# Silu moved to the reader's side of a round trip through DRAM, and products on two fixed pairs of PSUM banks

## The chip, the cores and the metric

The kernel runs on one core of a Trainium2 chip. The metric is the device time of one execution in microseconds, the median of several runs. All times below are microseconds unless marked ns.

## The reference

A recurrent linear attention (RetNet), followed by a feed-forward block with Silu. The inputs are float32 arrays for q, k and v (4 batches, 8 heads, 768 steps, 64 wide) and float64 weights, which the kernel converts itself.

```python
gamma = 1.0 - 2.0 ** (-5.0 - np.arange(H))
for t in range(S):
    state = gamma * state + k[:, :, t] (outer) v[:, :, t]
    y[:, :, t] = scale * (q[:, :, t] @ state)
x = y as (B*S, H*D) = (3072, 512)
h = x @ w_in                                  # (3072, 2048)
g = h * (1.0 / (1.0 + np.exp(-h)))            # Silu
out = g @ w_out                               # (3072, 512)
```

## The kernel before, in words

**Numbers.** The two big products are made of three products of fp32r parts each: an operand is split into a high part, a low part and a mixed part, and the sums of the first two and of the third go to two PSUM banks, `ha` and `hb` in the first half, `oa` and `ob` in the second. The result is `ONE_E * ha - hb`.

**Chunks, units, tiles.** The 768 steps are 6 chunks `c` of 128 steps; a unit is a chunk of one of the 4 batches, so there are 24 units. The width 2048 of the hidden layer is 16 slices `f` of 128. A product (c, f) of the first half (`multiply`, L749) multiplies a slice of w_in with the 512 columns (4 batches of 128 steps) of chunk c: 12 matmuls of 128x512, 8 into `ha` and then 4 into `hb` (L754).

**The first half.** The 96 products run in the order of the list `steps` (L1150), which is written out by hand, with the attention's work for the units (`visit` and `halves`, L690 to L739) put behind some of them. The first four products and the visits up to unit 10 or so stand in a hand-written order of their own (L968 to L1137). After a product, `close_steps` (L775) does three things: ACT copies `ha` to a buffer g and scales it (L777), DVE subtracts `hb` (L782), ACT applies Silu in place (L787). Then `put_g` (L792) has SP store g to DRAM (`g_dram`, L797). There are three g buffers (pool `hpool`); nine early products keep their g for longer in free weight slots (`new_g`, L764; their tile is called gk). While all this runs, ACT and DVE also convert and split the weights (L211 to L230, and L121 to L129) and do their part of the visits: xt (L653, L656, L659) is the attention's output, split in three parts, which the products of its chunk read.

**PSUM.** There are 8 banks: two each for the tags s and y, one for q, and three, h0 to h2, that `turn` (L403) hands out in rotation. Before the change `ha` and `hb` take the next two of the rotation. The bank of tag q is used by the transposes of the visits up to unit 13 (`steps_t`, L480), and those also take a turn. Later units are transposed by DMA (`turn_t`, L452; POOL separates the words for it, L444).

**The second half.** For each chunk and each f, `split` (L833) handles a g that SP loaded from DRAM four ahead (`get`, L803, L810): ACT writes the high part (L842), DVE the other two (L844, L845). The parts of four f are one block in a pool of two, so four Copies run together when TensorE has finished the block before the last. `split` runs 3 ahead of the matmuls: 12 of 128x512 per f (L1268), into 8 banks for 4 batches. At the end of a chunk ACT and DVE empty the banks (L1316, L1317), and SP stores the rows (L1244). The loads use 8 buffers in rotation (tags kf, qf and vf), so load n waits for the DVE subtraction (L844) of n - 8.

**What sets the order.** TensorE's order is the program's. On the other engines, from L1138 on, a scheduler orders the instructions; `tc.issue_after(ins)` makes those in its block queue behind `ins` if they are on the same engine. Names used for it: `copied[0]` is the newest L777, `taken_out[0]` the newest L782, `stored[0]` the newest store of a g.

Of the kernel before, what the change touches and what calls it, by code (L numbers as in the profile page):

```python
# [18 lines left out]
AF = mybir.ActivationFunctionType  # L19
# [15 lines left out]
def kernel(  # L35
# [28 lines left out]
    nc = tc.nc  # L64
# [17 lines left out]
    def pool(name, bufs, **kw):  # L82
# [14 lines left out]
    g_dram = {(c, f): dram.tile([128, NT], FP32, tag=f"g{c}_{f}", name=f"gd_{c}_{f}")  # L97
              for c in range(NC) for f in range(NF)}
# [40 lines left out]
    def woven(t, parted=False):  # L139

        if parted:
            return t.rearrange("p (h o n) -> p h n o", h=2, o=2)
        return t.rearrange("p (o n) -> p n o", o=2)
# [118 lines left out]
    def queue(ins):  # L262

        return ExitStack() if written[0] or ins is None else tc.issue_after(ins)
# [54 lines left out]
    def fill(out, n, start=True):  # L319

        cols = out.shape[-1] // 128
        for _ in range(n):
            nc.tensor.matmul(out, lhsT=zero, rhs=zero.unsqueeze(1).to_broadcast([128, cols, 128]),
                             start=start, stop=True, skip_group_check=True)
# [66 lines left out]
    taken_out, copied, masked, fenced = [], [], [], []  # L391
# [6 lines left out]
    def banks(tag, name, n=2):  # L398
        return ps_u.tile([128, n, 512], FP32, tag=tag, name=name)
# [3 lines left out]
    def turn(name):  # L403
        turns[0] += 1
        return ps_h.tile([128, 512], FP32, tag=f"h{turns[0] % 3}", name=name)
# [17 lines left out]
    def scale_k(n):  # L423
        if 0 <= n < len(units):
            t = kqv["k"][n]
            if units[n][0] == NC - 1:
                t = t[:D]
            g = gk[: t.shape[0], units[n][0], :].unsqueeze(2).to_broadcast([t.shape[0], H, D])
            engine = nc.gpsimd if 2 * B + 1 < n < FAR else nc.vector
            engine.tensor_tensor(out=t, in0=t, in1=g, op=ALU.mult)  # L430
# [27 lines left out]
    def join_t(name, n):  # L458

        to, bufs = (qt, 3) if name == "q" else (kt, 2)  # L460
        to[n] = one.tile([128, HP, C], FP32, tag=f"{name}t", name=f"{name}t_{n}", bufs=bufs)
        nc.scalar.copy(out=to[n].bitcast(U16).rearrange("p a (t w) -> p w a t", w=2),
                       in_=turned.pop((name, n)).rearrange("p (w a) t -> p w a t", w=2))
# [279 lines left out]
    apart = [(FAR + 1, "k"), (FAR + 1, "q"), (FAR + 2, "q")]  # L743
    pending, stored = [], []

    def product_in(c, f):
        close_in(c, f, *multiply(c, f))

    def multiply(c, f):  # L749
        ha, hb = turn(f"ha_{c}_{f}"), turn(f"hb_{c}_{f}")  # L750
        fill(ha, FILL_P.get((c, f), 0))
        for i in range(3):
            for kk in range(KIN):
                nc.tensor.matmul(hb if i == 2 else ha, lhsT=w_sb[f][:, i, ts(kk, 128)],  # L754
                                 rhs=woven(xt[c][:, i, kk, :]), start=kk == 0 and i != 1,
                                 stop=kk == KIN - 1 and i != 0)
        return ha, hb
# [6 lines left out]
    def new_g(c, f):  # L764
        if (c, f) not in kept_g:
            return hpool.tile([128, NT], FP32, tag="hs", name=f"g_{c}_{f}")
        i, = (i for i in keep_g if (c, f) in keep_g[i])
        if i not in homes:
            homes[i] = wpool.tile([128, 3, NT], FP32, tag=f"w{i}", name=f"gk_{i}")
        return homes[i][:, keep_g[i].index((c, f))]  # L770

    def close_in(*of):
        list(close_steps(*of))

    def close_steps(c, f, ha, hb):  # L775
        hs = new_g(c, f)
        copied[:] = [nc.scalar.activation(out=hs, in_=ha, func=AF.Copy, scale=ONE_E).ins]  # L777
        with queue(copied[0]):
            while behind_copy:
                behind_copy.pop(0)()  # L780
        yield
        taken_out[:] = [nc.vector.tensor_tensor(out=hs, in0=hs, in1=hb, op=ALU.subtract).ins]  # L782
        with queue(taken_out[0]):
            while behind_next:
                behind_next.pop(0)()
        yield
        nc.scalar.activation(out=hs, in_=hs, func=AF.Silu)  # L787
        (later if (c, f) in kept_g else pending).append((c, f, hs))

    later = []  # L790
# [1 line left out]
    def put_g(keep, of=None):  # L792
        of = pending if of is None else of
        while len(of) > keep:
            c, f, g = of.pop(0)
            with tc.issue_after(last[0]) if of is later else ExitStack():
                last[:] = stored[:] = [nc.sync.dma_start(out=g_dram[c, f], in_=g).ins]  # L797
# [5 lines left out]
    def get(n):  # L803
        if n >= len(order):
            return
        c, f = order[n]
        name = "kvqkvkqv"[n % 8]
        g = ld.tile([128, NT], FP32, tag=f"{name}f", name=f"gr_{c}_{f}",
                    bufs=2 if name == "q" else 3)
        nc.sync.dma_start(out=g, in_=g_dram[c, f])  # L810
        got[n] = g

    def get_w(f):
# [19 lines left out]
    def split(n):  # L833
        if n >= len(order):
            return
        c, f = order[n]
        get(n + G_AHEAD)
        g = got.pop(n)
        if f % 4 == 0:
            blocks[n // 4] = xpool.tile([128, 3, 4, NT], FP32R, tag="xt", name=f"gs_{c}_{f}")  # L840
        t = blocks[n // 4][:, :, f % 4, :]
        nc.scalar.activation(out=t[:, 0, :], in_=g, func=AF.Copy, scale=HALF)  # L842
        high = t[:, 0, :].bitcast(FP32)
        nc.vector.tensor_tensor(out=t[:, 1, :], in0=g, in1=high, op=ALU.subtract)  # L844
        nc.vector.scalar_tensor_tensor(out=t[:, 2, :], in0=t[:, 1, :].bitcast(FP32),  # L845
                                       scalar=-1.0 / EPS, in1=high,
                                       op0=ALU.mult, op1=ALU.add)
        ready[n] = t
# [294 lines left out]
    pairs = [(1, 1), (1, 2), (0, 3), (1, 3), (0, 4), (1, 4)]  # L1143
# [6 lines left out]
    steps = pairs + three + rest + last + groups  # L1150
# [32 lines left out]
    put_later = {6: 1, 7: 2, 9: 1, 10: 1, 11: 1, 13: 1, 14: 1, 15: 1}  # L1183
    assert sum(put_later.values()) == len(kept_g)
    loads_at = {first_far + 4: [("k", FAR + 1), ("q", FAR + 1)], far[FAR] + 1: [("q", FAR + 2)]}
    for n, (c, f) in enumerate(steps):
        if n in scales_at:
            behind_next.append(lambda m=scales_at[n]: scale_k(m))
        if n in joins_at:
            behind_copy.insert(0, lambda m=joins_at[n]: [join_t(name, m) for name in "qk"])  # L1190
        if n in parts:
            behind_next.append(lambda m=parts[n]: part_t(m, taken_out[0]))
        patient[0] = steps.index((3, 0)) <= n < max(turns_at) + 2
        product_in(c, f)
        put_g(1)
        if n in put_later:
            put_g(len(later) - put_later[n], later)
        store_w()
        if (c, f) in takes:
            take_w(taken_out[0], n < len(pairs + three) or c == NC - 1)  # L1200
        behind.get((c, f), lambda: None)()
        if n in turns_at:
            turn_t(turns_at[n])
            if turns_at[n] >= LATER:
                with tc.issue_after(turned_by[0]):
                    load("k", turns_at[n] + 1), load("q", turns_at[n] + 1)
        if turns_at.get(n - 1, 0) >= LATER:
            with tc.issue_after(stored[0]):
                load("v", turns_at[n - 1] + 1)
        if turns_at.get(n - 2, 0) >= LATER:  # L1210
            with tc.issue_after(stored[0]):
                while waiting:
                    load_w(waiting.pop(0))
        for name, m in loads_at.get(n, ()):
            load(name, m)
        if c == NC - 1:
            if f == 0:
                for i in range(W_READ):
                    get_w(i)
            if f < NF - 4:  # L1220
                w_out(f, True)
            if f >= NF - 6:
                if f == NF - 6:
                    for n in range(G_AHEAD):
                        get(n)
                if f >= NF - S_AHEAD:
                    with tc.issue_after(taken_out[0]):
                        split(f - NF + S_AHEAD)
# [6 lines left out]
    def unwoven(t):  # L1235

        return t.rearrange("p (n o) -> p o n", o=2)
# [8 lines left out]
    for c in range(NC):  # L1246
        acc = []
        for b in range(B):
            if b < 2:
                u = banks("sy"[b], f"o{b}_{c}")  # L1250
# [5 lines left out]
        for f in range(NF):  # L1256
            n = c * NF + f
# [3 lines left out]
            t = ready[n]  # L1261
# [13 lines left out]
        if early_f < NF:  # L1275
# [3 lines left out]
                         for x in ("left", "right")]  # L1279
            nc.scalar.activation(out=apart_cols(halves_of[0]),  # L1280
                                 in_=unwoven(acc[B - 1][0][:, left]), func=AF.Copy,
# [16 lines left out]
        for b in range(B):  # L1298
            oa, ob = acc[b]
            if c == NC - 1 and b == B - 1:  # L1300
# [4 lines left out]
                for i, (x, cols, op) in enumerate(((last_left, left, ALU.add),  # L1305
                                                   (oa, right, ALU.subtract))):
                    nc.vector.scalar_tensor_tensor(
                        out=apart_cols(o[i]), in0=unwoven(x[:, cols]), scalar=ONE_E,
# [44 lines left out]
```

## Time and profile before

| | |
|---|---|
| median of 3 runs | 601.49 (600.5 to 601.88) |
| profiled execution | 600.71 |
| its span | 598.7 |
| TensorE busy | 583.7 (97%) |
| VectorE (DVE) busy | 399.6 (67%) |
| ScalarE (ACT) busy | 333.2 (56%) |
| GpSimd (POOL) busy | 34.4 (6%) |
| DMA, share of 16 engines | 64.5% (main queue) |

The profile is of one execution; its span reaches from the first to the last instruction. PE is TensorE's matmuls, PEld its weight loads, which run beside them. A row of the groups gives line, engine, operation, output<-input, shapes and count, then busy time, mean ns of one, idle time of the engine just ahead and what ended it. A row of the timeline gives start, length, engine, line and, in brackets, the wait ahead of it and what ended the wait. A row of the waits gives the total, how often and the longest. Line numbers in rows are those of the kernel before.

### The profile page before, as it was taken

How to read it: one execution, taken by the hardware profiler on the slowest of the kernel's cores; microseconds unless marked ns; L12 is line 12 of the kernel's file. 1: busy time of each engine (PE TensorE's matmuls, PEld its weight loads, DVE VectorE, ACT ScalarE, POOL GpSimd, SP SyncE). 2: the span in 40 equal slices, each digit the busy share in tenths (PEclk: the TensorE clock that was granted, in tenths of full speed). 3: DMA queues.
4: the chain of work that ended last, by engine and by line, in shares of the span. 5: the costliest groups of instructions: out<-in, count | busy, mean ns of one | idle time of the engine just before them, and what ended most of it. 6: DMA issues, size and time to landing. Idle time of an engine off the chain costs nothing. (4 is left out here: it accounts for less than half of the span.)

```text
span 598.7 us, 13719 instructions
## 1 busy us (share of the span) xinstructions
PE 583.7 (97%) x5509; PEld 496.5 (83%) x5509; DVE 399.6 (67%) x672; ACT 333.2 (56%) x607; POOL 34.4 (6%) x89
## 2 busy tenths in 40 slices
PE   8999999999999999999999999999999999999997
PEld 6687887878778788878887888888888888888886
DVE  3888898777887767766679895553735544554632
ACT  7778878777867667777789761412312221413211
POOL 3000220100012111111000000000000000000000
PEclk9999999999999999999999999999999999999999
DMA  9997868785799689999977654352533524442301
GB/s 190 214 212 185 210 177 269 231 249 172 211 268 202 183 251 234 248 267 301 310 242 258 202 158 138 105 175 73 175 107 105 176 78 134 141 139 79 133 1 70
DMA packets 144334, 108.89 MB, mean 182 GB/s; under 512 B 101136, under 2 KB 109584, under 8 KB 144272
## 3 DMA queue, kind: packets, MB, share of 16 engines
q1 hardware_dynamic: 144272, 108.03, 64.5%
q8 instruction: 43, 0.70, 0.5%
q14 instruction: 19, 0.16, 0.1%
HBM read 66.06 MB, written 36.70 MB: 172 GB/s over the span
## 5 line engine op out<-in xcount | busy, mean ns | idle before, releaser
L754 PE MATMUL ha<-xt,wi 128*128 128x512 f32 x736 | 177.8, 384 | 1.0 <-DVE g L782 0.9
L754 PEld LDWEIGHTS ha<-xt,wi 128*128 128x128 f32 x736 | 136.0, 189 | 25.9 <-DVE g L782 6.4
L1268 PE MATMUL o<-wo,gs 128*128 128x512 f32 x564 | 137.1, 379 | 0.0
L842 ACT ACTIVATE gs<-gr 128x512 fp32r<-128x512 f32 x96 | 53.0, 619 | 130.2 <-issue 129.7
L1268 PEld LDWEIGHTS o<-wo,gs 128*128 128x128 f32 x564 | 106.6, 189 | 15.1
L844 DVE TENSOR_TENSOR gs<-gr,gs 128x512 fp32r<-128x512 f32 x96 | 62.3, 687 | 84.9 <-ACT gs L842 84.9
L1268 PE MATMUL oa<-wo,gs 128*128 128x512 f32 x376 | 111.8, 379 | 0.0
L754 PE MATMUL hb<-xt,wi 128*128 128x512 f32 x368 | 95.9, 383 | 4.9 <-ACT g L777 3.6
L782 DVE TENSOR_TENSOR g<-g,hb 128x512 f32<-128x512 f32 x87 | 59.6, 685 | 49.4 <-ACT g L777 46.0
L754 PEld LDWEIGHTS hb<-xt,wi 128*128 128x128 f32 x368 | 68.2, 189 | 19.3 <-ACT g L777 8.0
L1268 PEld LDWEIGHTS oa<-wo,gs 128*128 128x128 f32 x376 | 71.1, 189 | 10.1
L787 ACT ACTIVATE g<-g 128x512 f32<-128x512 f32 x87 | 54.6, 628 | 32.0 <-DVE g L782 31.9
L1268 PE MATMUL ob<-wo,gs 128*128 128x512 f32 x188 | 71.3, 379 | 0.0
L845 DVE SCALAR_TENSOR_TENSOR gs<-gs 128x512 fp32r<-128x512 f32 x96 | 62.2, 686 | 0.1
L777 ACT ACTIVATE g<-ha 128x512 f32<-128x512 f32 x87 | 51.2, 588 | 14.5 <-DMA gd<-g 11.0
L1268 PEld LDWEIGHTS ob<-wo,gs 128*128 128x128 f32 x188 | 35.5, 189 | 5.0
L211 ACT ACTIVATE ca<-wf 128x512 f32<-128x512 f32 x32 | 26.7, 835 | 12.6 <-DVE cs L224 7.0
L1316 ACT ACTIVATE o<-o 128x512 f32<-128x512 f32 x10 | 6.0, 600 | 31.1 <-PE o L1268 30.9
L224 DVE SCALAR_TENSOR_TENSOR cs<-ca,cs 128x512 uint32<-128x512 uint32 x32 | 22.4, 701 | 0.9
L659 DVE SCALAR_TENSOR_TENSOR xt<-xt 128x512 fp32r<-128x512 f32 x28 | 22.1, 800 | 0.6
L542 DVE TENSOR_TENSOR am<-sc,decay 128x512 f32<-128x512 f32 x24 | 16.5, 687 | 8.0 <-PE sc L534 6.9
L582 PE MATMUL y<-qt,mid 64*64 64x64 f32 x376 | 19.4, 220 | 0.6 <-issue 0.6
(137 smaller groups left out, 615.9 us busy)
## 6 DMA issues: line engine op xcount, KB each, us to landing
gr<-gd SPq DMA_DIRECT2D x96, 256.0 KB, 2.8
gd<-g SPq DMA_DIRECT2D x87, 256.0 KB, 3.4
wf<-in_moe_w_out_dram SPq DMA_DIRECT2D x16, 512.0 KB, 5.2
out_dram<-o SPq DMA_DIRECT2D x23, 256.0 KB, 2.5
wf<-in_moe_w_in_dram SPq DMA_DIRECT2D x16, 256.0 KB, 4.0
wf<-in_moe_w_in_dram SPq DMA_DIRECT2D x32, 128.0 KB, 3.9
kf<-in_k_dram SPq DMA_DIRECT2D x16, 256.0 KB, 4.4
qf<-in_q_dram SPq DMA_DIRECT2D x16, 256.0 KB, 4.9
```

The lines of the kernel that those rows point to most:

```text
L211: top = nc.scalar.activation(out=a.bitcast(FP32), in_=hi.bitcast(FP32), func=AF.Abs, scale=2.0 ** -3).ins
L224: nc.vector.scalar_tensor_tensor(out=s, in0=a, scalar=3, in1=s, op0=ALU.logical_shift_left, op1=ALU.bitwise_xor)
L582: i = nc.tensor.matmul(to[ts(e, D), o, a, :], lhsT=lhsT, rhs=rhs, start=key not in started, stop=True, skip_group_check=True).ins
L659: nc.vector.scalar_tensor_tensor(out=x[2], in0=x[1].bitcast(FP32), scalar=-1.0 / EPS, in1=x[0].bitcast(FP32), op0=ALU.mult, op1=ALU.add)
L754: nc.tensor.matmul(hb if i == 2 else ha, lhsT=w_sb[f][:, i, ts(kk, 128)], rhs=woven(xt[c][:, i, kk, :]), start=kk == 0 and i != 1, stop=kk ...
L777: copied[:] = [nc.scalar.activation(out=hs, in_=ha, func=AF.Copy, scale=ONE_E).ins]
L782: taken_out[:] = [nc.vector.tensor_tensor(out=hs, in0=hs, in1=hb, op=ALU.subtract).ins]
L787: nc.scalar.activation(out=hs, in_=hs, func=AF.Silu)
L842: nc.scalar.activation(out=t[:, 0, :], in_=g, func=AF.Copy, scale=HALF)
L844: nc.vector.tensor_tensor(out=t[:, 1, :], in0=g, in1=high, op=ALU.subtract)
L845: nc.vector.scalar_tensor_tensor(out=t[:, 2, :], in0=t[:, 1, :].bitcast(FP32), scalar=-1.0 / EPS, in1=high, op0=ALU.mult, op1=ALU.add)
L1268: nc.tensor.matmul(o, lhsT=g, rhs=woven(wo[f][:, i, :], (c, b) == (NC - 1, B - 1)), start=f == 0 and i != 1, stop=f == NF - 1 and i != 0 o ...
```

## The change

The Silu behind a product's subtraction goes away, so g is stored without it, and the second half applies Silu in place on the loaded g, ahead of the Copy of its high part; it is queued behind the newest copy of the first half. The loads of g are queued behind the newest store of a g. From the product behind unit 13's visit on (the 86 steps after `pairs`), products take their banks by turns: the even ones two of the rotation, the odd ones one of the rotation and the bank of tag q.

```diff
+    home_of = {}
+
     def multiply(c, f):
-        ha, hb = turn(f"ha_{c}_{f}"), turn(f"hb_{c}_{f}")
+        names = f"ha_{c}_{f}", f"hb_{c}_{f}"
+        home = home_of.get((c, f), "t")
+        if home in "sy":
+            u = banks(home, names[0])
+            ha, hb = (u[:, i] for i in range(2))
+        else:
+            ha = turn(names[0])
+            hb = banks("q", names[1], 1)[:, 0] if home == "q" else turn(names[1])
...
     def close_steps(c, f, ha, hb):
...
         yield
-        nc.scalar.activation(out=hs, in_=hs, func=AF.Silu)
         (later if (c, f) in kept_g else pending).append((c, f, hs))
...
     def get(n):
...
-        nc.sync.dma_start(out=g, in_=g_dram[c, f])
+        with tc.issue_after(stored[0]):
+            nc.sync.dma_start(out=g, in_=g_dram[c, f])
...
     def split(n):
...
         t = blocks[n // 4][:, :, f % 4, :]
+        with tc.issue_after(copied[0]):
+            nc.scalar.activation(out=g, in_=g, func=AF.Silu)
         nc.scalar.activation(out=t[:, 0, :], in_=g, func=AF.Copy, scale=HALF)
...
+    home_of.update({x: "tq"[n % 2] for n, x in enumerate(steps[len(pairs) :])})
     for n, (c, f) in enumerate(steps):
```

The homes s and y, which `multiply` can also take, are given to no product here.

## Prediction

> **What bounds the kernel now.** I read the stage table first (busy time of each engine in stretches; its clock column stands before the DMA share).
>
> ```profile
> 80.00:345.50 265.50, 260.30 (x2588) 218.65 (x2587) 203.61 (x341) 201.96 (x331) 24.43 (x34) 1.00 0.86 240
> 345.50:595.00 249.50, 248.83 (x1157) 217.83 (x1155) 134.80 (x221) 68.52 (x126) 0.00 (x0) 1.00 0.36 116
> ```
>
> Columns: length, then busy PE, PEld, DVE, ACT, POOL, granted clock, DMA share, GB/s. The first row is the products of the first half with the attention visits between them, the second the second half. TensorE is full in both, at clock 1.00. In the first row ACT and DVE are busy three quarters of the time; in the second ACT is at 27%.
>
> The chain of work shows whether a full TensorE is at its pace. First and last of the 88 pieces from one whole step of the second half to another:
>
> ```profile
> 345.66 1.29 PE o L1268 x6
> 348.25 1.29 PE o L1268 x6
> ...
> 573.58 1.29 PE o L1268 x6
> ```
>
> (573.58 - 345.66) / 88 = 2.59 us a step, and each step has 12 matmuls of 128x512: 0.216 us each, without one late step. So the second half has nothing to give; this change can only take there. A product of the first half has 12 matmuls of the same form. Its pace, from the timeline of PE:
>
> ```profile
> 120.04 1.89 PE L754 MATMUL ha<-xt,wi 128*128 128x512 f32 x8
> ...
> 122.63 1.89 PE L754 MATMUL ha<-xt,wi 128*128 128x512 f32 x8
> ...
> 125.22 1.89 PE L754 MATMUL ha<-xt,wi 128*128 128x512 f32 x8
> 127.78 1.13 PE L754 MATMUL hb<-xt,wi 128*128 128x512 f32 x4 [0.68 <-ACT g L777]
> 128.75 1.89 PE L754 MATMUL ha<-xt,wi 128*128 128x512 f32 x8
> ```
>
> Two products are 2.59 apart, then one takes 128.75 - 125.22 = 3.53: 0.94 lost, because hb's bank was still unread. The weight loader's waits give the sum of such losses:
>
> ```profile
> PEld hb L754 <- ACT g L777: 8.0, 14, 1.8
> PEld ha L754 <- DVE g L782: 6.4, 18, 0.8
> ```
>
> 14.4 us in 32 waits. The loader runs ahead of PE, so a wait costs a little less than it lasts; for the product above its own row is
>
> ```profile
> 127.78 0.73 PEld L754 LDWEIGHTS hb<-xt,wi 128*128 128x128 f32 x4 [1.08 <-ACT g L777]
> ```
>
> 1.08 of waiting, 0.94 lost: 0.14 less. 14.4 - 32 x 0.14 = **9.9 us** is what the banks cost, all in "g" products, which are those from unit 13's visit on and one before.
>
> Why they are late: three banks turn. Product n's hb takes the bank of ha(n-1), so ACT's copy (L777) of the product just before must be out; its ha takes the bank of hb(n-2), so DVE's subtraction (L782). And ACT is behind:
>
> ```profile
> 151.09 0.64 ACT L121 ACTIVATE wi<-cs 128x512 fp32r<-128x512 f32 x1
> 151.60 0.63 ACT L787 ACTIVATE g<-g 128x512 f32<-128x512 f32 x1
> 152.12 0.59 ACT L777 ACTIVATE g<-ha 128x512 f32<-128x512 f32 x1
> 152.60 0.63 ACT L127 ACTIVATE wi<-wil 128x512 fp32r<-128x512 f32 x1
> ```
>
> Back to back, with a Silu (L787) in front of a copy that PE waits for.
>
> **The change part by part.** (a) *Four banks.* Products alternate between pair (turn, turn) and pair (turn, q). Two products take three turns, so each keeps its banks: ha(n) now waits for the copy of n-2, hb(n) for the subtraction of n-2. The copy gets 12 - 8 = 4 matmuls more (0.86 us), the subtraction 8 more (1.73 us). All ha waits (longest 0.8) lie under 1.73. Of the hb waits one lies over 0.86, the longest:
>
> ```profile
> 261.55 1.89 PE L754 MATMUL ha<-xt,wi 128*128 128x512 f32 x8
> ...
> 264.17 0.62 ACT L777 ACTIVATE g<-ha 128x512 f32<-128x512 f32 x1
> 264.84 0.73 PEld L754 LDWEIGHTS hb<-xt,wi 128*128 128x128 f32 x4 [1.80 <-ACT g L777]
> ```
>
> The copy ends at 264.79; the next ha would be due at 261.55 + 2.59 = 264.14 and now waits for it: 0.65 and some 0.1 for the restart stay, 0.75. The wait of 1.08 leaves 1.08 - 0.86 = 0.22, if ACT is no quicker. q is free then: unit 13's is the last visit that transposes on PE.
>
> (b) *Silu leaves the first half.* By groups:
>
> ```profile
> L787 ACT ACTIVATE g<-g 128x512 f32<-128x512 f32 x87 | 54.6, 628 | 32.0 <-DVE g L782 31.9
> L787 ACT ACTIVATE gk<-gk 128x512 f32<-128x512 f32 x9 | 5.7, 630 | 4.4 <-DVE gk L782 4.3
> L842 ACT ACTIVATE gs<-gr 128x512 fp32r<-128x512 f32 x96 | 53.0, 619 | 130.2 <-issue 129.7
> ```
> ```profile
> PEld y L582 <- ACT gk L787: 0.3, 1, 0.3
> ```
>
> 96 Silus, 60.3 us, leave ACT; in the first stage it falls from 76% to about 57%, so copies come earlier by up to 0.63 each. The store of g waits for the subtraction alone, so a g buffer comes free sooner, though SP's order stays nearly the same. I count (b) as what makes (a) hold while PE runs faster, with no sum of its own; in the stage before unit 13, where Silus also go, one wait of 0.3 is ended by one (last row): a gain of 0 to 1, as others wait behind ACT, taken as 0.
>
> *What is late next.* DVE keeps its work, 203.6 us, now in about 256: 80%. Three things stay: the wait above (0.75), some 0.3 for xt parts around 91 us, and this one:
>
> ```profile
> 169.85 2.97 DVE L659 SCALAR_TENSOR_TENSOR xt<-xt 128x512 fp32r<-128x512 f32 x2
> 172.97 1.10 PE L754 MATMUL hb<-xt,wi 128*128 128x512 f32 x4 [0.64 <-DVE xt L659]
> ```
>
> It isn't a bank's (two such instructions take 2.97, beside two copies on POOL). If PE comes 5 us sooner and this chain doesn't, it grows by up to 5; the chain hangs on subtractions of the products before, which come sooner too (at 152.12 a copy is 2 us late). I take it as unchanged, with 0 to 2 more as its range. First-half gain: 9.9 - 0.75 - 0.3 = 8.85, and 0 to 0.3 from restarts: **9.0**.
>
> (c) *Silu in the second half*, in place on gr, same form as L787: 96 x 0.63 = 60.3 more on ACT, 68.5 becomes 129 of 249.5 us. It adds queue order, no semaphore: Silu behind the newest first-half copy, each gr load on SP behind the newest store. Two places count.
>
> *The start.* The first four Copies into gs ran early; they now stand between the last products, after copies 13, 14, 15:
>
> ```profile
> 339.85 0.58 ACT L777 ACTIVATE g<-ha 128x512 f32<-128x512 f32 x1
> 341.30 0.63 ACT L787 ACTIVATE g<-g 128x512 f32<-128x512 f32 x1 [0.87 <-DVE g L782]
> 342.30 0.60 ACT L777 ACTIVATE g<-ha 128x512 f32<-128x512 f32 x1 [0.36 <-PE ha L754]
> ...
> 344.88 0.60 ACT L777 ACTIVATE g<-ha 128x512 f32<-128x512 f32 x1 [0.37 <-PE ha L754]
> ```
>
> Step 0 is due at 345.50: copy ends 340.43, Silu 0.63, Copy 0.62, two DVE operations of 0.69: 343.1. Step 1, after the copy at 342.30: 345.5 against 348.1. Step 2, after the copy at 344.88, with two Silus and two Copies and DVE: 349.8 against 350.7. The next block is due at 355.9 and starts with ACT free at 348: nothing is late.
>
> *The chunk ends*, five of them, where ACT must empty the accumulators (L1316). ACT's new order there: four Copies (L842), the Silus of four loads that those Copies' buffers let go, then L1316.
>
> ```profile
> 378.21 3.33 SPq L810 DMA_DIRECT2D gr<-gd  x4
> 379.90 1.29 DVE L844 TENSOR_TENSOR gs<-gr,gs 128x512 fp32r<-128x512 f32 x2
> 385.20 1.25 ACT L1316 ACTIVATE o<-o 128x512 f32<-128x512 f32 x2 [6.18 <-PE o L1268]
> 385.83 1.34 DVE L1317 TENSOR_TENSOR o<-o,o 128x512 f32<-128x512 f32 x2 [3.43 <-ACT o L1316]
> 386.55 2.60 SPq L1244 DMA_DIRECT2D out_dram<-o  x4
> ```
> ```profile
> DMA to landing us min/median/max: 2.7/2.8/2.9
> ...
> DMA to landing us min/median/max: 2.5/2.8/4.7
> ```
>
> The last of the four loads goes out when the last L844 has read its buffer, 379.90 + 1.29 = 381.19, lands 2.8 later (first landing row: the four loads at the second chunk end; second: all of the second half), its Silu ends at 384.62; L1316 is ready at 385.20: 0.58 in hand. The first subtraction ends at 386.52, and PE needs that bank two matmuls into the next chunk (345.50 + 16 x 2.59 + 0.43 = 387.4): 0.9 more. So 1.4 us in hand, and the cost is **0**. Each us of lateness beyond that costs 5.
>
> Sum: span 598.7 - 9.0 = 589.7. The profiled run took 600.71, 2.0 more than its span, so 591.7; it lay 0.8 under the median of 601.49: **592.5**.
>
> A rule of the Trainium skill speaks against (c): "ScalarE: Activation LUTs", section "Table sets: the hidden batching unit", wants activations grouped by table set, since each change of set costs a load. The case's trace has one load ahead of its first Silu and none after, though 96 Silus alternate with Copy and Abs:
>
> ```profile
> L919 ACT ACT_TABLE_LOAD x1 | 1.3, 1283 | 0.0
> ```
>
> By the rule alone the sum would be that of the last rival below; by the row it is 0.
>
> **The rivals.** *Partly given back:* weights, xt, DVE or a g buffer is late in place of the bank. For it: copies wait for stores of g, 11.0 us in 10 waits.
>
> ```profile
> ACT g L777 <- DMA gd<-g: 11.0, 10, 2.4
> ```
>
> Against it: most of these end before PE asks for the bank, and it has 0.86 more. Half the gain: 597.
>
> *Slower:* at the chunk ends a Silu waits for its load and holds L1316 behind it. It decides from a landing of 2.8 + 1.4 = 4.2 us on, and beats the gain from 4.2 + 9.0 / 5 = 6.0; at 6.6 us it costs 5 x 2.4 = 12: 604.5. Against it: landings of 2.7 to 2.9 there, 4.7 at most anywhere in the half.
>
> *It does nothing:* PE would have waited anyway, for what the bank hid; 601.5.
>
> *Table loads:* if Silu and Copy changed sets, some 16 changes around 341 to 357 of 1.283 each are 20 us, less some 7 of room: 592.5 + 13 = 605.5.
>
> **How the numbers follow.** Forecast 0.68 (590 to 594.5), partly given back 0.16 (594.5 to 599), nothing 0.05, slower by the chunk ends or a queue like it 0.10, table loads 0.01. Low end: 9.9, 1 from the stage before unit 13, 0.64 and 0.3 for xt, 11.8 in all, and the spread of the runs: 589. High end 598.5 takes in most of the partial case and leaves out 0.17. Faster by over 0.2% (1.2 us, about what a measurement here can tell from none): 0.68 + 0.16 = 0.84; within 0.05; slower 0.11.
>
> **What would show it.** The two PEld rows on g should fall from 14.4 to under 3; products from 100 to 335 us should stand 2.59 apart but for one near 260 and one near 170; the second half should begin near 336.5 and stay at 2.59 a step. L1316 should start as late after its chunk as now. Wrong: new PEld waits on wi or xt, gaps at the chunk ends, or a late step 2.

## The result and the profile after

| | before | after |
|---|---|---|
| median | 601.0 (4 runs, 599.77 to 601.88) | 594.5 (4 runs, 593.44 to 596.02) |
| profiled execution | 600.71 | 595.38 |
| its span | 598.7 | 593.6 |
| start of the first product's matmuls to that of the last (c = 5, f = 15) | 26.73 to 342.91 | 26.77 to 337.50 |
| last matmul of the program starts | 594.06 | 588.64 |

Faster: ratio 0.9895, 95% interval [0.9863, 0.9928], 6.5 us by the medians. A later series gave 0.988 [0.9853, 0.9906]. In the traces all of it comes from the first half: its last product starts 5.4 us sooner, and from there to the last matmul both kernels take 251.14 us.

New lines stand for old ones: the matmuls of a product L763 (was L754), the copy out of the bank L786 (L777), the subtraction L791 (L782), Silu L852 (L787), Copies of the second half L853 (L842), the emptying of a chunk's banks L1328 (L1316), the second half's matmuls L1280 (L1268).

The stage table of the kernel after, cut where its first half ends, in the columns of the prediction's first fence:

```profile
80.00:340.10 260.10, 255.72 (x2588) 220.84 (x2587) 201.30 (x338) 157.51 (x245) 24.42 (x34) 1.00 0.87 240
340.10:589.90 249.80, 248.81 (x1157) 217.82 (x1155) 137.08 (x225) 126.45 (x222) 0.00 (x0) 1.00 0.37 121
```

The same matmuls take 5.4 us less in the first half. ACT's 202 us there are now 158, and its 69 us in the second half are 126.

The weight loader's waits after, those on a product's banks and on xt:

```profile
PEld ha L763 <- ACT g L786: 3.2, 3, 1.8
PEld hb L763 <- DVE gk L791: 1.7, 2, 0.8
PEld ha L763 <- DVE xt L656: 1.5, 2, 0.8
PEld hb L763 <- DVE xt L659: 1.3, 1, 1.3
...
PEld ha L763 <- ACT xt L653: 0.6, 1, 0.6
...
PEld hb L763 <- DVE g L791: 0.2, 1, 0.2
```

The two rows on g had 14.4 us in 32 waits before; they have 3.4 in 4. The rows on xt have grown: 0.5 in the waits before (and 0.64 that TensorE itself waited), 3.4 now. The products that the prediction showed 3.53 apart now keep their pace, on the timeline of PE after:

```profile
122.11 1.89 PE L763 MATMUL ha<-xt,wi 128*128 128x512 f32 x8
...
124.70 1.89 PE L763 MATMUL ha<-xt,wi 128*128 128x512 f32 x8
...
127.29 1.89 PE L763 MATMUL ha<-xt,wi 128*128 128x512 f32 x8
```

The second half, by the first and the last of 94 pieces on the chain of work after:

```profile
340.25 1.29 PE o L1280 x6
...
581.12 1.29 PE o L1280 x6
```

(581.12 - 340.25) / 93 = 2.59 us a step, as before. And its chunk ends, by ACT's rows for the first and the last of them:

```profile
379.78 1.25 ACT L1328 ACTIVATE o<-o 128x512 f32<-128x512 f32 x2 [0.63 <-PE o L1280]
...
545.54 1.25 ACT L1328 ACTIVATE o<-o 128x512 f32<-128x512 f32 x2 [0.60 <-PE o L1280]
```

ACT is there 0.6 us ahead of TensorE (0.55 to 0.63 at the five ends), where it used to be 6.2 ahead.

So far all looks as forecast, two thirds of the size. The experiments say that it came about otherwise.

### The profile page after: what moved, and what is told of

Same layout as the page of the kernel before. It is cut to its first block, busy times and chain, and to the rows that moved or that the text cites. A ratio compares the mean times of both kernels' runs of the same rounds, so it can differ in the third digit from the quotient of the medians.

```text
span 593.6 us, 13695 instructions
## 1 busy us (share of the span) xinstructions
PE 578.8 (98%) x5509; PEld 498.3 (84%) x5509; DVE 400.7 (68%) x672; ACT 343.1 (58%) x607; POOL 33.3 (6%) x89
## 4 chain that ended last, share of the span: by engine, by line
PE 71%; DVE 11%; DMA 7%; ACT 5%; issue 3%; SPq 2%; POOL 0%; DVEq 0%; ACTq 0%; POOLq 0%
PE o L1280 21%; PE ha L763 16%; PE oa L1280 14%; PE hb L763 8%; PE ob L1280 7%; PE y L582 2%; DMA gd<-g 2%; DVE cs L224 1%; SPq L172 1%; DVE xt L656 1%; DVE cs L214 1%; DVE g L791 1%; DMA wf<-in_moe_w_out_dram 1%; DMA wod<-cw 1%; DMA kqv<-in_q_dram 1%
## 5 line engine op out<-in xcount | busy, mean ns | idle before, releaser
L763 PE MATMUL ha<-xt,wi 128*128 128x512 f32 x736 | 176.6, 382 | 3.1 <-ACT g L786 1.9
L763 PEld LDWEIGHTS ha<-xt,wi 128*128 128x128 f32 x736 | 137.2, 189 | 24.9 <-ACT g L786 3.2
L1280 PE MATMUL o<-wo,gs 128*128 128x512 f32 x564 | 137.1, 379 | 0.0
L1280 PEld LDWEIGHTS o<-wo,gs 128*128 128x128 f32 x564 | 106.6, 189 | 15.1
L1280 PE MATMUL oa<-wo,gs 128*128 128x512 f32 x376 | 111.8, 379 | 0.0
L852 ACT ACTIVATE gr<-gr 128x512 f32<-128x512 f32 x96 | 59.6, 628 | 65.9 <-DMA gr<-gd 64.8
L763 PE MATMUL hb<-xt,wi 128*128 128x512 f32 x368 | 94.8, 380 | 1.8 <-DVE xt L659 0.9
L791 DVE TENSOR_TENSOR g<-g,hb 128x512 f32<-128x512 f32 x87 | 59.6, 685 | 44.6 <-ACT g L786 33.8
L786 ACT ACTIVATE g<-ha 128x512 f32<-128x512 f32 x87 | 51.8, 597 | 64.6 <-PE ha L763 36.5
L763 PEld LDWEIGHTS hb<-xt,wi 128*128 128x128 f32 x368 | 69.2, 189 | 12.9 <-DVE gk L791 1.7
L1280 PEld LDWEIGHTS oa<-wo,gs 128*128 128x128 f32 x376 | 71.1, 189 | 10.1
L853 ACT ACTIVATE gs<-gr 128x512 fp32r<-128x512 f32 x96 | 53.2, 620 | 37.2 <-PE ob L1280 28.9
L1280 PE MATMUL ob<-wo,gs 128*128 128x512 f32 x188 | 71.3, 379 | 0.0
L1280 PEld LDWEIGHTS ob<-wo,gs 128*128 128x128 f32 x188 | 35.5, 189 | 5.1
L211 ACT ACTIVATE ca<-wf 128x512 f32<-128x512 f32 x32 | 26.5, 828 | 21.8 <-DVE cs L224 11.8
L659 DVE SCALAR_TENSOR_TENSOR xt<-xt 128x512 fp32r<-128x512 f32 x28 | 20.5, 744 | 0.6
L1329 DVE TENSOR_TENSOR o<-o,o 128x512 f32<-128x512 f32 x10 | 6.7, 687 | 17.4 <-ACT o L1328 17.4
```

The costliest lines, as they stand in the source:

```text
L211: top = nc.scalar.activation(out=a.bitcast(FP32), in_=hi.bitcast(FP32), func=AF.Abs, scale=2.0 ** -3).ins
L659: nc.vector.scalar_tensor_tensor(out=x[2], in0=x[1].bitcast(FP32), scalar=-1.0 / EPS, in1=x[0].bitcast(FP32), op0=ALU.mult, op1=ALU.add)
L852: nc.scalar.activation(out=g, in_=g, func=AF.Silu)
L1280: nc.tensor.matmul(o, lhsT=g, rhs=woven(wo[f][:, i, :], (c, b) == (NC - 1, B - 1)), start=f == 0 and i != 1, stop=f == NF - 1 and i != 0 o ...
```

## The experiments: which part gives the gain

Each ratio is to the kernel before, run beside it in the same series (three series, in which its medians were 602.8, 602.69 and 602.48). The theory, from the prediction: the banks give the gain, the moved Silu none of its own. The rival: it is ScalarE's relief.

**The banks alone.** The kernel before with the new banks:

```diff
     def close_steps(c, f, ha, hb):
...
         yield
+        nc.scalar.activation(out=hs, in_=hs, func=AF.Silu)
...
     def get(n):
...
-        with tc.issue_after(stored[0]):
-            nc.sync.dma_start(out=g, in_=g_dram[c, f])
+        nc.sync.dma_start(out=g, in_=g_dram[c, f])
...
     def split(n):
...
-        with tc.issue_after(copied[0]):
-            nc.scalar.activation(out=g, in_=g, func=AF.Silu)
```

(shown against the kernel after; its Silu is L796)

> Only the banks are changed: Silu stays in the first half, behind each product's subtraction, and the loads of the second half are placed as before. Theory (the banks give the gain, the moved Silu has no sum of its own): 594 to 596, and the waits of the weight loads on the copies and subtractions of g fall from 14.4 us to under 5. Rival (ScalarE rid of 0.63 us a product in the first half is what the time came from): 600 to 601.5, those waits above 10 us.

Measured: 603.75, ratio 1.0007 [0.9983, 1.0032]: no gain. All instructions stand in the same order on every engine as in the kernel before; only the banks differ. Of the waits left in its trace, one of 2.4 us at 228 us is behind a weight conversion that waits for its load, and TensorE's half pace behind it (last section) costs 1.7 more.

**Silu alone.** The kernel after, with every product back on the three banks in rotation:

```diff
-    home_of.update({x: "tq"[n % 2] for n, x in enumerate(steps[len(pairs) :])})
```

> Only Silu is moved to the second half; every product uses the banks that it had before. Theory (banks give the gain): 599 to 601, the waits on copies and subtractions of g stay at 11 to 14.4 us, some of the copies 0.6 us sooner. Rival (ScalarE's relief gives it): 594 to 596, those waits under 6 us. In both the second half is as long as in the changed kernel, within 0.5 us.

Measured: 593.24, ratio 0.9825 [0.9793, 0.9857]; a second series of it, below, gave 593.31, 0.985 [0.9822, 0.9878]. The theory has fallen: the moved Silu gives the whole gain. The order is the same as in the kernel after on every engine, so these two also differ in the banks alone. Against the kernel before, moving Silu also moves the loads of g, and the scheduler changes SP's order in some other places. The loads are not the main cause: product (4, 4) starts 6.2 us sooner than in the kernel before, of 7.6 at the last product, and the first such load of the kernel before goes out only behind that, at 272.69 us. The other changes of order were not tried alone.

The waits show why. The kernel with the banks alone, first the weight loader's:

```profile
PEld ha L763 <- ACT g L786: 10.0, 14, 2.4
...
PEld hb L763 <- DVE g L791: 0.4, 1, 0.4
```

The 14.4 us have become 10.4: no longer `hb` waits for the copy of the product just before, but `ha` for the copy of the one before that. What the copies wait for stands in ACT's own rows. Before:

```profile
ACT g L787 <- DVE g L782: 31.9, 37, 2.6
ACT g L777 <- DMA gd<-g: 11.0, 10, 2.4
...
ACT g L777 <- PE ha L754: 2.5, 7, 0.4
```

With the banks alone:

```profile
ACT g L796 <- DVE g L791: 30.6, 37, 2.4
ACT g L786 <- DMA gd<-g: 10.9, 10, 3.0
...
ACT g L786 <- PE ha L763: 1.7, 4, 0.5
```

With Silu alone moved:

```profile
ACT g L786 <- PE ha L763: 56.5, 45, 2.4
ACT g L786 <- DMA gd<-g: 9.1, 4, 3.0
```

Read the row in which the copy waits for PE: before, it lasts 2.5 us in 7 waits, that is, out of 87 copies only 7 waited for TensorE; 10 more waited for a store to free their buffer. Most others came late because ACT was behind, and the room of 0.86 us is used up after a few products: over the 86 products from (0, 5) on, the copy starts 1.39 us behind the product's first `hb` matmul before (median; 0.20 is as early as it usually can), 2.16 with the banks alone and 0.20 with Silu alone. (In the first rows, ACT stands at Silu until DVE has subtracted, 32 us in all, with the next copy queued behind it.) With Silu gone ACT waits for PE 56.5 us: it has time in hand, and three banks do. The weight loader's rows on g of that kernel:

```profile
PEld ha L763 <- DVE g L791: 2.3, 6, 0.8
...
PEld hb L763 <- ACT g L786: 0.8, 2, 0.5
```

3.1 us (3.4 in its second series), no more than with four banks.

**ScalarE's time, or its standing at Silu?** The moved Silu took two things from ACT: 0.63 us of work a product, and the wait for DVE ahead of it. Two kernels are meant to give back one each, both on the kernel with Silu alone moved.

```diff
         copied[:] = [nc.scalar.activation(out=hs, in_=ha, func=AF.Copy, scale=ONE_E).ins]
+        copied[:] = [nc.scalar.activation(out=hs, in_=hs, func=AF.Copy, scale=1.0).ins]
```

> Silu alone moved, banks as before, and in the first half one more ScalarE instruction a product: a Copy of the 128x512 tile g onto itself (no change of values), directly behind the copy out of the bank, so that it waits for nothing. It gives ScalarE back the 0.6 us a product that the move took away, and holds the subtraction 0.6 us, but not the wait for VectorE. Theory (what costs is ScalarE standing with Silu at the head of its queue until VectorE has subtracted, with the next copy behind it): 592 to 595. Rival (ScalarE's busy time is what costs): 599 to 602.

```diff
         yield
+        nc.scalar.activation(out=hs[:, :1], in_=hs[:, :1], func=AF.Copy, scale=1.0)
         (later if (c, f) in kept_g else pending).append((c, f, hs))
```

> Silu alone moved, banks as before, and in the first half, where Silu stood behind each subtraction, a Copy of one column of g onto itself (128x1, no change of values): ScalarE waits for VectorE as with Silu, and the store waits for ScalarE, but only some 0.2 us of work stand there. Theory (the wait at the head of the queue costs): 599 to 602. Rival (busy time costs): 592 to 595.

Measured: work without the wait 605.74, ratio 1.006 [1.0038, 1.0082]; the wait with little work 596.69, ratio 0.9916 [0.9891, 0.9942]. Neither theory stands alone. The group of the small instruction, from the groups of ACT in the second kernel, and the loader's rows there:

```profile
L796 ACT ACTIVATE g<-g 128x1 f32<-128x1 f32 x87 | 17.3, 199 | 34.4 <-DVE g L791 33.9
```
```profile
PEld hb L763 <- ACT g L786: 4.5, 7, 1.2
PEld ha L763 <- DVE g L791: 4.1, 10, 0.7
```

ACT stands as long as at Silu (33.9 us), with a third of its work (0.199 of 0.63 us), and loses 0.0066 to 0.0091 of the time against Silu alone, some 4.0 to 5.5 us of the 9 to 10.5 that Silu costs in its old place. So the wait and the first 0.2 us are about half of Silu's price. The store of g waits for the small instruction as it did for Silu, and that part is not separated. That the rest of the work is the other half is by subtraction, not shown. The first kernel is no clean test of the work: its Copy stands ahead of the subtraction and delays it, which the loader's row there shows (14.8 us in 24 waits, where Silu in its old place had 6.4):

```profile
PEld ha L763 <- DVE g L792: 14.8, 24, 1.2
```

**A fourth buffer for g**, on Silu alone:

```diff
-            return hpool.tile([128, NT], FP32, tag="hs", name=f"g_{c}_{f}")
+            return hpool.tile([128, NT], FP32, tag="hs", name=f"g_{c}_{f}", bufs=4)
...
-        mid = one.tile([128, HP, D], FP32, tag="mid", name=f"mid_{n}", bufs=2)
+        mid = one.tile([128, HP, D], FP32, tag="mid", name=f"mid_{n}", bufs=1)
...
-            state[b] = one.tile([128, HP, D], FP32, tag="state", name=f"state_{n}", bufs=B + 2)
+            state[b] = one.tile([128, HP, D], FP32, tag="state", name=f"state_{n}", bufs=B + 1)
```

(`ys`, of the same pool, has four as well)

> Silu alone moved, banks as before, and four buffers for g in place of three; to make room, mid has one buffer in place of two and state five in place of six. Theory (what is left of late copies comes from waiting for the store of g three products before): 590 to 592, the row of copies waiting for stores near 0. Rival (those waits end before TensorE asks for the bank): 592.5 to 594, as with three; the smaller mid and state could cost something.

Measured: 593.36, ratio 0.9849 [0.982, 0.9878]. The copies no longer wait for stores of g at all, and nothing is gained: it looks as if, with three banks and Silu gone, those waits were over before TensorE asked. The smaller `mid` and `state` could hide a small gain, and a fourth buffer on the kernel before was not tried.

## The experiments: the second half, and where the lead goes

**Twice the addition to the second half**, on the kernel after:

```diff
             nc.scalar.activation(out=g, in_=g, func=AF.Silu)
+            nc.scalar.activation(out=g, in_=g, func=AF.Copy, scale=1.0)
```

> The changed kernel with one more ScalarE instruction behind each Silu of the second half, a Copy of the same 128x512 tile onto itself (no change of values), so that what the move adds to that half is doubled: 96 x 0.6 us more. Theory (the second half is set by TensorE, and the chunk ends have 1.4 us in hand): 594.5 to 595.5, last matmul at most 1 us later. Rival (the chunk ends already stand on the edge): 0.6 us at each of the five chunk ends and at the start, 597.5 to 598.

Measured: 602.0, ratio 0.9964 [0.9939, 0.999]. From the last product's start to the last matmul it takes 257.6 us in place of 251.14. The rival was right about this kernel, and the price is larger than its 3 us. The worst chunk end of it, on the timeline (Silu is L852, the added Copy L853, the emptying L1329 and L1330):

```profile
384.27 0.61 ACT L852 ACTIVATE gr<-gr 128x512 f32<-128x512 f32 x1
384.91 0.63 ACT L853 ACTIVATE gr<-gr 128x512 f32<-128x512 f32 x1
385.45 1.06 ACT L1329 ACTIVATE o<-o 128x512 f32<-128x512 f32 x2
...
386.80 2.13 PE L1281 MATMUL o<-wo,gs 128*128 128x512 f32 x6 [2.98 <-DVE o L1330]
```

ACT is full from the loads on, comes late to the banks, and TensorE waits 3 us. So the addition as it is costs nothing, with the 0.6 us shown above in hand; doubled, with some four more instructions of 0.62 us ahead of L1329, it makes the weight loader wait 5.0 us in the five ends, 3.4 of it in this one, and half pace behind that wait (last section) adds 1.5. The half is free, and not by much.

**Once more the two kernels that differ in banks alone**, unaltered, since Silu alone seemed the faster:

> The changed kernel once more, unaltered, to stand beside the Silu-alone kernel (ratio 0.9825 to before). All instructions of the two stand in the same order on every engine; only the banks differ. If four banks cost something on top of the moved Silu: ratio 0.988 to 0.992, that is 594.5 to 597 where before has 602. If they make no difference and the first comparison was the spread of runs: 0.981 to 0.985, 590.5 to 593.

> Silu alone moved, once more, unaltered. The changed kernel has stood at 0.9895 and 0.988 of before, this one at 0.9825. If the four banks really cost something on top: 0.981 to 0.985. If the first result was the spread: 0.987 to 0.990.

Measured: the changed kernel 594.77, ratio 0.988 [0.9853, 0.9906]; Silu alone 593.31, 0.985 [0.9822, 0.9878]. With the first series that is 594.5 and 594.8 against 593.2 and 593.3. The intervals overlap by little; the banks cost some 1.4 us, if anything, and gain nothing. The traces show a place for it. The start of five products, the first of them the first with the new banks:

| product | before | after | after, second series | Silu alone | Silu alone, second |
|---|---|---|---|---|---|
| (0, 5) | 85.22 | 85.13 | 84.84 | 86.30 | 85.34 |
| (1, 15) | 165.52 | 160.96 | 160.66 | 163.24 | 162.65 |
| (2, 10) | 178.65 | 175.58 | 174.74 | 176.24 | 175.73 |
| (3, 12) | 238.05 | 235.10 | 234.05 | 234.08 | 234.00 |
| (4, 4) | 265.81 | 261.75 | 260.82 | 259.62 | 259.14 |

With four banks TensorE takes 75.8 us from (0, 5) to (1, 15) in both traces, with three 76.9 and 77.3: it gains 1.1 to 1.5. At (3, 12) none of that is left, and at (4, 4) it is behind. The wait there, in the kernel after:

```profile
253.22 0.41 SPq L196 DMA_DIRECT2D wf<-in_moe_w_out_dram  x1
...
259.23 0.88 ACT L211 ACTIVATE ca<-wf 128x512 f32<-128x512 f32 x1 [4.09 <-DMA wf<-in_moe_w_out_dram]
...
261.11 1.08 ACT L786 ACTIVATE g<-ha 128x512 f32<-128x512 f32 x2
...
261.75 1.99 PE L763 MATMUL ha<-xt,wi 128*128 128x512 f32 x8 [1.35 <-ACT g L786]
```

A conversion (L211) waits 4.1 us for its weight at the head of ACT's queue, two copies stand behind it, and TensorE waits for the first.

**That conversion, later.** On the kernel after, so that ACT doesn't get to it before the weight:

```diff
-    takes += [(3, f) for f in (0, 3, 7, 11, 14)]
-    takes += [(4, f) for f in (0, 3, 7, 11, 14)]
+    takes += [(3, f) for f in (0, 5, 8, 11, 14)]
+    takes += [(4, f) for f in (2, 5, 8, 11, 14)]
```

> The changed kernel with four conversions of an output weight taken two products later or one (third chunk: product 5 in place of 3 and 8 in place of 7; fourth chunk: 2, 5, 8 in place of 0, 3, 7), so that ScalarE does not reach the conversion before its weight has landed. Theory (the 0.58 us at 222.42 and the 1.51 us at 261.75 that are left come from copies standing behind that waiting conversion): 592 to 593. Rival (the copies are late for another reason, above all buffers of g): no change, 594 to 595, and the waits stay or move to the next visit.

Measured: 596.09, ratio 0.9869 [0.9839, 0.99], no better than the kernel after. The wait at 262 us is gone, and two like it come, by ACT's timeline at 271.56 and 285.25:

```profile
271.56 0.89 ACT L211 ACTIVATE ca<-wf 128x512 f32<-128x512 f32 x1 [3.75 <-DMA wf<-in_moe_w_out_dram]
...
285.25 0.88 ACT L211 ACTIVATE ca<-wf 128x512 f32<-128x512 f32 x1 [4.58 <-DMA wf<-in_moe_w_out_dram]
```

The load moves with the conversion, since it waits for the buffer that an earlier one frees (these loads wait 14.0 us in all, in 8 waits, for DVE's last step on an earlier weight).

**Fewer weights midway**, on the kernel after:

```diff
-    takes += [(4, f) for f in (0, 3, 7, 11, 14)]
-    takes += [(5, f) for f in (2, 5, 8)]
+    takes += [(4, f) for f in (7, 11, 14)]
+    takes += [(5, f) for f in (0, 2, 4, 6, 8)]
```

> The changed kernel (with its four banks), two of the output-weight conversions moved from the fourth chunk to the fifth: products 7, 11, 14 in place of 0, 3, 7, 11, 14, then 0, 2, 4, 6, 8 in place of 2, 5, 8. Each conversion loads 512 KB and stores 256 KB, so 1.5 MB leave the stretch from 160 to 280 us, where the DMA engines are busy 0.88 to 1.04 of the time, for the one from 280 to 335, where they are at 0.76. Theory (the full DMA engines take back what TensorE has gained when it gets there): 591.5 to 593.5, the wait at 260 us under 0.5. Rival (the lead is lost to the order of ScalarE's queue, not to the amount moved): 594 to 595.5.

Measured: 597.99, ratio 0.9921 [0.9892, 0.9949], slower. At 262 us it did what it should: product (4, 4) begins at 259.57, where the kernel after had 261.75. But in the last chunk of the first half, where the wo parts for the second half are made as well, the copies come late again: 4.4 us in four waits of the loader (0.76, 1.84, 0.31 and 1.46) between 317 and 340 us.

**xt earlier**, on the kernel after:

```diff
-    behind[0, NF - 2] = lambda: [late_y(b) for b in range(2)]
-    behind[1, NF - 4] = lambda: [late_x(0), late_y(2), late_x(1), late_y(3)]
-    behind[1, NF - 2] = lambda: [late_x(2), late_x(3)]
+    behind[0, NF - 3] = lambda: [late_y(b) for b in range(2)]
+    behind[0, NF - 1] = lambda: [late_x(0), late_y(2), late_x(1), late_y(3)]
+    behind[1, NF - 3] = lambda: [late_x(2), late_x(3)]
```

> The changed kernel with the third chunk's last part of xt loaded and split one product earlier (loads of y behind product 13 of the first chunk in place of 14, the splits behind 15 of the first and 13 of the second in place of 12 and 14 of the second). Theory (that chain costs 2 us at 166 to 170 us since TensorE comes sooner and the chain does not): those waits fall from 2.8 to under 1, and 592.5 to 593.5 if the lead lasts. Rival (the DMA engines are full from 160 to 280 us and take the lead back): the waits at 166 to 170 go, those at 199, 222 and 262 grow, 594 to 595.5.

Measured: 592.99, ratio 0.9842 [0.9815, 0.9868]. The waits on xt at 166 to 170 us are gone, and product (2, 10) begins at 173.23 (after: 175.58 and 174.74). Product (2, 14) begins at 190.13, where the second series of the kernel after had 190.19: all is given back in one visit. Its timeline:

```profile
180.49 3.13 SPq L455 DMA_TRANSPOSE qw<-qp  x1
...
185.49 0.60 ACT L786 ACTIVATE g<-ha 128x512 f32<-128x512 f32 x1 [4.09 <-DMA gd<-g]
...
186.72 0.68 DVE L656 TENSOR_TENSOR xt<-y,xt 128x512 fp32r<-128x512 f32 x1
...
187.55 0.69 PE L582 MATMUL y<-am,vf 64*64 64x64 f32 x32 [1.47 <-DVE xt L656]
```

SP's queue is held by a transpose, a store of g and so a copy come late, DVE's queue behind it, and TensorE waits for the bank of y that L656 reads. This kernel is 1.8 us faster by the medians than the kernel after in its second series, but the intervals overlap; 1.0 us of it is in the traces, and comes from the wait at 262 us, 0.24 lost in place of 1.2, a place that the edit doesn't touch. The rival was right at the place, the theory about the time.

**Both edits on Silu alone:**

> Silu alone moved, banks as before, with both of the other edits: two output-weight conversions from the fourth chunk to the fifth, and the third chunk's xt one product earlier. If both places still cost something there: 590 to 592. If three banks hide them anyway: 592.5 to 594, as with Silu alone.

Measured: 598.91, ratio 0.9936 [0.9914, 0.9958]; TensorE loses 2.9 us in four gaps between 320 and 339 us, the place where the late conversions cost in the kernel above.

Why a lead is lost between 175 and 235 us is argued, not shown. The stage from 160 to 280 us of the kernel after speaks for the transfers:

```profile
160.00:280.00 120.00, 115.97 (x1677) 98.68 (x1679) 87.41 (x146) 65.86 (x93) 20.18 (x28) 1.00 0.98 242
280.00:340.00 60.00, 60.00 (x436) 52.53 (x429) 46.74 (x79) 38.26 (x68) 0.09 (x1) 1.00 0.75 245
```

The DMA engines are busy 0.98 of it, and the copies wait 25.0 us for stores of g in the whole of the kernel after and 22.2 in its second series (9.1 and 12.7 with Silu alone). A kernel that moves less data there with everything else in place was not tried. Of the versions measured, Silu alone (593.2 and 593.3), xt earlier on the kernel after (593.0) and four g buffers (593.4) are the best, and not told apart.

## Why the prediction was right in the sum and wrong in the part

*The range and the side* held: 594.5 in 589.0 to 598.5, 2.0 above the forecast. The gain is 6.5 us where 9.0 were forecast. That the sum came out so near was luck: the part that it rests on gives nothing alone, and the part that it put at nothing gives it all.

*"9.9 us is what the banks cost"*: as a size this was right. Every gap between the starts of two matmuls that is over 0.216 us and lies beside one of those 32 waits, summed by what it is over, gives 10.1 us in the trace of before.

*"(a) Four banks"* is the step that failed. The slack was worked out rightly and set against each wait as if the copies' lateness were given from outside. It isn't: most copies were late because ACT's queue hardly ever emptied, and the banks alone leave 10.4 us of such waits and 1.0007 of the time. The waits on a bank were a sign of how late ACT was, not of too few banks. The Trainium skill, "Perfetto Trace Analysis", section "Optimization Strategy", says that the same gap again and again on the engine that should be full can mean too few buffers or banks for the next tile. The gaps here were of that kind, and with a fourth bank 10.4 of 14.4 us stayed: here the measurement speaks against that reading.

*"(b) ... no sum of its own"* failed with it. It is worth 9 to 10.5 us (ratios 0.9825 and 0.985), about half of it ACT's standing at Silu for DVE with 0.2 us of work behind it, which the prediction's own group of Silu had as idle time (32.0 us) and which it didn't price. The rows that would have told were at hand: the copy waits for PE in 7 of 87 cases.

*"What is late next"*: the wait left near 262 us was there, but it lost 1.6 us where 0.75 was forecast, behind a conversion that waited for its weight. The xt chain at 170 us was taken as unchanged with up to 2 more in the range; the matmuls' delays around the waits on xt, summed as above, are 1.2 us before and 3.2 after. The waits on g that are left, at 199, 222 and 262 us, lose 2.8 us (summed so) where 0.75 was allowed. So 10.1 - 2.8 = 7.3 went on g and 2.0 came back on xt: 5.3, the 5.4 of the traces.

*"The cost is 0"* for the second half: right, with the 0.58 us in hand that was forecast for L1316 measured as 0.55 to 0.63. The rival of chunk ends had the right place: twice the work shows nearly all of its 6.5 us there.

*The start of the second half* was due at 336.5 and came at 340.1, by the lead that was lost. *Table loads*: after, too, one load ahead of the attention's first activations and one more early on, and none beside the 96 moved Silus, so that rival is out. The rule that the prediction set against (c) did not bear on it. The section of the Trainium skill that it cites, in "ScalarE: Activation LUTs", also counts copy and abs among the functions that are in every set, and the trace agrees.

*Partly given back*, at 0.16, is what the trace after looks like, with a weight, xt and g buffers late in place of the bank; the median of 594.5 lies on the border that was drawn between it and the forecast.

## What to carry to other kernels

Before giving a waiting engine more buffers, look whether the engine it waits for ever waits in turn: where it hardly does (2.5 us in 7 of 87 here), more buffers may only move the wait, and less work there may remove it. An instruction at the head of an in-order queue costs its wait as well as its work, for all that stands behind it. A place that is free as measured may be free by half a microsecond: double the addition and see.

## What the hardware showed beside that

After some pauses TensorE ran at half its pace. In the kernel with the banks alone, on the timeline of PE and then by the stage table (clock in the third column from the end):

```profile
225.36 1.03 PE L763 MATMUL hb<-xt,wi 128*128 128x512 f32 x4
228.33 3.62 PE L763 MATMUL ha<-xt,wi 128*128 128x512 f32 x8 [1.95 <-ACT g L786]
...
232.71 1.89 PE L763 MATMUL ha<-xt,wi 128*128 128x512 f32 x8
```
```profile
225.00:229.00 4.00, 2.05 (x9) 1.45 (x8) 0.69 (x2) 2.91 (x5) 0.00 (x0) 0.94 0.51 184
229.00:233.00 4.00, 4.00 (x13) 3.20 (x13) 3.90 (x8) 2.71 (x5) 0.00 (x0) 0.63 0.88 172
```

Behind a wait of 1.95 us eight matmuls stand 0.43 us apart, 3.4 us in place of 1.7. With the second half's work doubled, the same comes behind the wait of 2.98 us, after four gaps of 0.22 to 0.32: seven of 0.43. A wait of 1.8 us in that same kernel, at 263 us, has none of it, and neither has the wait of 1.35 us in the kernel after. So a wait of 2 us can cost nearly as much again (1.7 us behind the 1.95), and one of 3 us half as much again (1.5), which no step of the prediction had; what decides is not shown. The Trainium skill, "TensorE: Matmul & The Clock Gate", section "What's actually happening", has a window of 3413 ns that runs on its own and half the clock after at least one idle window. The length of the slow stretch, 3.4 us, agrees; that it follows a wait of only 1.95 us does not.
